# Top-32 attention and a token/channel mixer on one core: the mask of two tiles in three moved to GpSimd as a saturated 0-or-1 word, the dummy values moved to ScalarE

## The chip, the cores and the metric

The kernel runs on 1 core of one Trainium2 chip. The engines of the core are named as the profile names them: PE (TensorE matmul) and PEld (its weight loads), DVE (VectorE), ACT (ScalarE), POOL (GpSimd) and SP (SyncE, which here only issues DMAs). The metric is the device time of one execution in microseconds (us). All inputs and outputs are float32; the kernel itself uses float32 for the scores and bfloat16 behind them.

## The reference

For 8 batches of 8 heads, with 576 positions and a head width of 64:

```python
scores = scale * np.matmul(q, k.transpose(0, 1, 3, 2))        # 576 x 576 per head
kth = np.partition(scores, -32, axis=-1)[..., -32:-31]
mask = scores >= kth
attn = softmax of the masked scores
x = np.matmul(attn, v)                                        # heads side by side: 576 x 512 per batch
h = np.maximum(x.T @ w_tok1, 0.0) @ w_tok2
u = x + h.T
out = u + np.maximum(u @ w_ch1, 0.0) @ w_ch2
```

So each row of scores keeps its 32 largest, takes the exponentials of these, normalises and mixes the values. Two small networks follow, one along the positions and one along the channels.

## The kernel before

**Tiles.** Two heads make a pair; a pair has 9 tiles of 128 score rows by 576 columns (four for each head, and one that holds the last 64 rows of both). 32 pairs make 288 tiles. After the fourth pair of a batch the mixer of that batch (`mlp_ops`) is put beside the attention of the next batch.

**A tile** (`tile_ops`, from line 441) goes round the engines:
- PE makes the scores (L370, L362 for the tile of the last rows) into a two-bank PSUM tile, `big`, of which there are three. ACT copies them to `Ssb` in SBUF (L447), of which there are eight.
- DVE takes the 8 largest of each of seven segments (L452) and reduces these candidates in five steps (L457 to L467) to `thi`, whose last entry is the 24th largest candidate: a first bound for the 32nd score.
- ACT writes `sg`, the sign of (bound - score), and with it the sum of the signs, `cnt` (L469 and its accumulator read). From `cnt` follows how many scores (24 to 31) lie above the bound.
- POOL writes `X` = score times sign (L473), in which the scores above the bound are negative.
- DVE writes the dummy values behind the 576 scores of `X` (L475): nine values, of which as many are +2^100 as the rank needs, the others very negative. The 8 largest of scores and dummies (L479, over 588 columns) then end in the exact 32nd score, `tlo`.
- The mask takes one of three forms, chosen by the tile's number modulo 9:

```python
form = (0, 0, 1, 0, 0, 2, 0, 0, 1)[i % 9]
```

Form 0 (192 tiles): ACT puts the exponential into a PSUM tile `big` (L484), and DVE compares and multiplies in one instruction (L486). Form 1 (64 tiles): ACT puts the exponential into `E` in SBUF (L490), DVE makes the negated bound `nt` (L494), POOL makes the mask in two passes, `Z` (L497: subtract and scale by 2^100) and `M` (L500: cut to 0 and 1), and multiplies (L507). Form 2 (32 tiles): POOL compares in one pass (L504) and multiplies (L507).
- SP issues a DMA transpose of the result `Pm` to `PT` (L509). When a head has its five, PE multiplies by the values (L400) and DVE normalises (L420 to L432).

**Order of the work.** Nothing is ordered while the kernel runs. `Plan` is a list scheduler that is run when the kernel is built: every operation is added with its engine, an assumed duration, a due time in units of `T` (3.1 us a tile), the operations it depends on and the buffers it takes and frees. `Plan.run` simulates the engines and gives one order, in which all instructions are issued; each engine then works through its own queue in that order and waits where data or a buffer isn't there. The loads of a pair are due 16 `T` ahead of it.

**At the end** DVE checks over all tiles that the counts and bounds were as assumed (L618 to L635). If not, an exact version of the whole (`exact_batch`) runs over the output.

Of the kernel before, what the change touches and what calls it, by code (L numbers as in the profile page):

```python
# [7 lines left out]

P = 128
TOPK = 32  # L10
NEG = -1.0e30
BIG = float(2.0**100)

CUT = 8396807.0 / 8388608.0
NSEG = 7
RANK_BASE = 24
NDUM = 9


class Buf:  # L20
# [135 lines left out]
def kernel(  # L156
# [23 lines left out]
    scale = 1.0 / float(D) ** 0.5  # L180
# [3 lines left out]
    ST = S - SM  # L184
    NPAIR = B * H // 2
    NT = NPAIR * 9
    XW = S + 12
    bounds = [round(i * S / NSEG) for i in range(NSEG + 1)]

    main = ExitStack()  # L190
# [3 lines left out]
    def sbt(name, shape, dt):  # L194
        return sb.tile(shape, dt, name=name, tag=name)
# [4 lines left out]
    plan = Plan()  # L200

    def slots(tag, n, shape, dt, psum=False):
        ts = [(pst if psum else sbt)(f"{tag}{i}", shape, dt) for i in range(n)]
        plan.tag(tag, ts)
        return ts

    identF = sbt("identF", [P, P], f32)
    identB = sbt("identB", [P, P], bf16)
    kdum = sbt("kdum", [P, 3, 4], f32)
    w1b = sbt("w1b", [P, 5, DT], bf16)  # L210
    w2b = sbt("w2b", [P, NJ, S], bf16)
    wc1b = sbt("wc1b", [P, NC, DC], bf16)
# [13 lines left out]
    slots("cd", 4, [P, NSEG, 8], f32)  # L226
    slots("m8", 6, [P, 8], f32)
    slots("nt", 4, [P, 1], f32)
    slots("Z", 2, [P, S], f32)
    slots("sg", 3, [P, S], bf16)  # L230
    Xs = slots("X", 4, [P, XW], f32)
    slots("M", 4, [P, S], bf16)
    Ps = slots("Pm", 4, [P, 5 * P], bf16)
    slots("PT", 18, [P, 5, P], bf16)
    slots("rd", 2, [P, 2, 5], f32)
# [11 lines left out]
    make_identity(nc, identF[:, :])  # L247
    nc.vector.tensor_copy(out=identB[:, :], in_=identF[:, :])
    for j in range(NDUM):
        nc.vector.memset(kdum[:, j // 3, j % 3 : j % 3 + 1], float(2 * (j + 1) - 529))  # L250
    for t in Xs:
        nc.vector.memset(t[:, S:XW], -BIG)
    for t in qLs:
        nc.vector.memset(t[:, 4, :, :], 0.0)
    for t in vbs:
# [1 line left out]
    for t in Ps:  # L257
        nc.vector.memset(t[:, S : 5 * P], 0.0)

    T = 3.1  # L260

    def load_w():
        nc.gpsimd.dma_start(
# [20 lines left out]
    def pair_ops(p):  # L284
        b, h0 = divmod(p, 4)
        h0 *= 2
        t0 = 9 * p * T
        qL, kL, vL, vb = Buf("qL"), Buf("kL"), Buf("vL"), Buf("vb")
        qT, kT = Buf("qT"), Buf("kT")
# [31 lines left out]
        pq, pk = Buf("big"), Buf("big")  # L321
# [12 lines left out]

        tt = t0 - 6 * T
        oq = plan.add("PE", 0.6, tt, tr(pq, qL, 5), [lq], acq=[pq, qT], use=[qL])
        ok = plan.add("PE", 0.6, tt + 0.5 * T, tr(pk, kL, 4), [lk], acq=[pk, kT], use=[kL])

        def cp(dst, src, n):
            return lambda: nc.scalar.copy(out=dst.t[:, 0:n], in_=src.t[:, 0:n])  # L340

        eq = plan.add("ACT", 0.65, tt + T, cp(qT, pq, 5 * P), [oq], use=[pq, qT])
        ek = plan.add("ACT", 0.6, tt + 1.5 * T, cp(kT, pk, S), [ok], use=[pk, kT])

        def cv():
            nc.scalar.copy(
# [61 lines left out]
        X = xb[b]  # L408
        tv = t0 + (9 + 5) * T
        for h in range(2):  # L410
# [26 lines left out]
            acq = [rd]  # L437
# [3 lines left out]
    def tile_ops(i, s, S_, om):  # L441

        E, cd, m8 = Buf("E"), Buf("cd"), Buf("m8")
        sg, X, M, Pm, PT = Buf("sg"), Buf("X"), Buf("M"), Buf("Pm"), Buf("PT")
        t = T * i

        ev = plan.add("ACT", 0.6, t + 0.6 * T, lambda: nc.scalar.copy(out=S_.t[:, :], in_=s.t[:, 0:S]),  # L447
                      [om], use=[s, S_])
        last = None
        segs = []  # L450
        for a in range(NSEG):
            segs.append(plan.add("DVE", 0.146, t + T + 0.01 * a, lambda a=a: nc.vector.max(  # L452
                cd.t[:, a, :], S_.t[:, bounds[a] : bounds[a + 1]]), [ev], acq=[cd] if a == 0 else [], use=[S_, cd]))
        d = segs

        def r1():
            nc.vector.max(m8.t[:, :], cd.t[:, :, 0:2])  # L457

        def cut(n):
            return lambda: nc.vector.match_replace(cd.t[:, :, 0:n], m8.t[:, :], cd.t[:, :, 0:n], NEG)  # L460

        tr = t + 1.6 * T
        a1 = plan.add("DVE", 0.085, tr, r1, d, acq=[m8], use=[cd])
        a2 = plan.add("DVE", 0.15, tr + .01, cut(2), [a1], use=[cd, m8])
        a3 = plan.add("DVE", 0.1, tr + .02, lambda: nc.vector.max(m8.t[:, :], cd.t[:, :, 0:5]), [a2], use=[cd, m8])
        a4 = plan.add("DVE", 0.17, tr + .03, cut(5), [a3], use=[cd, m8])
        a5 = plan.add("DVE", 0.125, tr + .04, lambda: nc.vector.max(thi[:, i, :], cd.t[:, :, :]), [a4], use=[cd])  # L467

        ct = plan.add("ACT", 0.77, t + 2.2 * T, lambda: nc.scalar.activation(  # L469
            out=sg.t[:, :], in_=S_.t[:, :], func=AF.Sign, scale=-CUT, bias=thi[:, i, 7:8],  # L470
            accum_out=cnt[:, i : i + 1]), [a5], acq=[sg], use=[S_])

        xm = plan.add("POOL", 1.31, t + 2.7 * T, lambda: nc.gpsimd.tensor_tensor(  # L473
            out=X.t[:, 0:S], in0=S_.t[:, :], in1=sg.t[:, :], op=ALU.mult), [ct], acq=[X], use=[S_, sg])
        dm = plan.add("DVE", 0.09, t + 3.3 * T, lambda: nc.vector.tensor_scalar(  # L475
            out=X.t[:, S:XW].rearrange("p (a b) -> p a b", a=3)[:, :, 0:3], in0=kdum[:, :, 0:3],
            scalar1=cnt[:, i : i + 1], scalar2=-BIG, op0=ALU.add, op1=ALU.mult), [ct, xm], use=[X])

        m = plan.add("DVE", 0.68, t + 3.4 * T, lambda: nc.vector.max(tlo[:, i, :], X.t[:, 0:XW]), [dm, xm], use=[X])  # L479
        thr = tlo[:, i, 7:8]  # L480
        form = (0, 0, 1, 0, 0, 2, 0, 0, 1)[i % 9]
        if form == 0:
            Ep = Buf("big")
            ex = plan.add("ACT", 0.6, t + 3.2 * T, lambda: nc.scalar.activation(  # L484
                out=Ep.t[:, 0:S], in_=S_.t[:, :], func=AF.Exp, scale=scale), [ev, xm], acq=[Ep], use=[S_])
            pm = plan.add("DVE", 0.7, t + 3.6 * T, lambda: nc.vector.scalar_tensor_tensor(  # L486
                out=Pm.t[:, 0:S], in0=S_.t[:, :], scalar=thr, in1=Ep.t[:, 0:S], op0=ALU.is_ge, op1=ALU.mult),
                [m, ex], acq=[Pm], use=[S_, Ep])
        else:
            ex = plan.add("ACT", 0.6, t + 2.4 * T, lambda: nc.scalar.activation(  # L490
                out=E.t[:, :], in_=S_.t[:, :], func=AF.Exp, scale=scale), [ev], acq=[E], use=[S_])
            if form == 1:
                nt, Z = Buf("nt"), Buf("Z")
                tn = plan.add("DVE", 0.07, t + 3.5 * T, lambda: nc.vector.tensor_scalar(  # L494
                    out=nt.t[:, :], in0=thr, scalar1=-(1.0 - 2.0**-24), scalar2=None, op0=ALU.mult),
                    [m], acq=[nt])
                z = plan.add("POOL", 0.8, t + 3.7 * T, lambda: nc.gpsimd.tensor_scalar(  # L497
                    out=Z.t[:, :], in0=S_.t[:, :], scalar1=nt.t[:, :], scalar2=BIG, op0=ALU.add, op1=ALU.mult),
                    [tn], acq=[Z], use=[S_, nt])
                mk = plan.add("POOL", 0.8, t + 3.71 * T, lambda: nc.gpsimd.tensor_scalar(  # L500
                    out=M.t[:, :], in0=Z.t[:, :], scalar1=1.0, scalar2=0.0, op0=ALU.min, op1=ALU.max),
                    [z], acq=[M], use=[Z])
            else:
                mk = plan.add("POOL", 2.0, t + 3.7 * T, lambda: nc.gpsimd.tensor_scalar(  # L504
                    out=M.t[:, :], in0=S_.t[:, :], scalar1=thr, scalar2=None, op0=ALU.is_ge),
                    [m], acq=[M], use=[S_])
            pm = plan.add("POOL", 1.31, t + 3.9 * T, lambda: nc.gpsimd.tensor_tensor(  # L507
                out=Pm.t[:, 0:S], in0=E.t[:, :], in1=M.t[:, :], op=ALU.mult), [mk, ex], acq=[Pm], use=[E, M])
        dt = plan.add("SP", 0.06, t + 4.5 * T, lambda: nc.sync.dma_start_transpose(  # L509
            out=PT.t[:, :, :], in_=Pm.t[:, :]), [pm], acq=[PT], use=[Pm], dma=1.3)  # L510
        return PT, dt
# [96 lines left out]
    for o in order:  # L608
# [4 lines left out]
    tmp = sbt("tmp", [P, NT], f32)  # L613
# [8 lines left out]
                                   op0=ALU.mult, op1=ALU.not_equal)  # L622
# [3 lines left out]
    nc.vector.tensor_reduce(out=bad[:, 1:2], in_=tmp[:, :], op=ALU.max, axis=AX.X)  # L626
    nc.vector.tensor_scalar(out=bad[:, 1:2], in0=bad[:, 1:2], scalar1=56.0, scalar2=None, op0=ALU.is_gt)
    nc.vector.tensor_tensor(out=tmp[:, :], in0=thi[:, :, 7], in1=tlo[:, :, 7], op=ALU.is_gt)
    nc.vector.scalar_tensor_tensor(out=tmp[:, :], in0=tlo[:, :, 7], scalar=0.0, in1=tmp[:, :],
                                   op0=ALU.is_gt, op1=ALU.mult)  # L630
    nc.vector.tensor_reduce(out=bad[:, 2:3], in_=tmp[:, :], op=ALU.min, axis=AX.X)
    nc.vector.tensor_scalar(out=bad[:, 2:3], in0=bad[:, 2:3], scalar1=0.5, scalar2=None, op0=ALU.is_lt)
# [7 lines left out]
    def exact_batch(b, pools):  # L640
        sp, pp = pools
        Xb = sp.tile([P, 5, C], bf16, name="fX", tag="fX")
        for h in range(H):
# [24 lines left out]
            for t in range(5):  # L668
# [92 lines left out]
    with tc.If(wrong > 0):  # L761
        with ExitStack() as fs:
# [10 lines left out]
                out=fw1[:, 0:4, :], in_=moe_w_tok1[0:SM, :].rearrange("(t p) c -> p t c", p=P)  # L773
# [39 lines left out]
```

## Time and profile before

| what | value |
|---|---|
| median of 2 runs | 1094.57 us (1092.71 to 1096.43) |
| the profiled execution's own time | 1090.94 us |
| its span, from the first to the last instruction | 1089.2 us |
| mean granted TensorE clock | 0.761 |
| HBM read, written | 35.78 MB, 9.44 MB |
| longest group of waits, POOL's product L473 for ACT's sign L469 | 333.2 us, 176 times |
| ACT's sign L469 for DVE's bound `thi` L467 | 170.7 us, 163 times |
| PE's score matmuls L370 for ACT's copy L447, for DVE's L486 | 67.2 us, 46.5 us |
| DVE's segment maxima L452 for ACT's copy L447 | 28.5 us, of which 26.8 is the start |

A group's line in the profile gives the line of the kernel, the engine, the operation, what it writes and reads, the shapes and the count; behind the first bar stand the busy time in us and the mean duration of one in ns, behind the second the idle time of the engine just before it and what ended it. Durations of neighbouring instructions on DVE and ACT overlap, so that a group's durations can add up to more than the engine's busy time. In the order of time each line has the start, the duration, and the instruction. The idle time of an engine that doesn't set the end costs nothing.

### The profile page before, as it was taken

The numbers are of one execution on the slowest core, as the hardware profiler recorded it, in microseconds if no ns is written. First come the engines' busy times: TensorE is split into PE (matmuls) and PEld (weight loads), VectorE is DVE, ScalarE is ACT, GpSimd is POOL, SyncE is SP. The second block draws the span as 40 slices with busy tenths as digits, with TensorE's granted clock in tenths as the row PEclk, the third lists the DMA queues.
The fourth block names the chain that finished last, engine by engine and source line by source line (L and its number), as shares of the span: only waits on it lengthen the run. The fifth ranks groups of instructions, "written<-read, shape, count | busy, mean of one in ns | idle before, by whom it ended". The sixth has DMA issues, their size and how long they took to land. (4 is left out here: it accounts for less than half of the span.)

```text
span 1089.2 us, 19075 instructions
## 1 busy us (share of the span) xinstructions
PE 834.2 (77%) x4804; PEld 480.0 (44%) x4850; DVE 988.6 (91%) x5094; ACT 735.6 (68%) x1465; POOL 636.0 (58%) x555
## 2 busy tenths in 40 slices
PE   2776678888789588897689876887787975798377
PEld 1443444555444354544455443444444543454233
DVE  0889999999999989999999999999999999999920
ACT  0766666876687766876678766787668866787422
POOL 1366666666765655566666665566556665665600
PEclk9756557995599755996589965898569966798578
DMA  9644334454435534454443543345434433234201
GB/s 178 134 67 88 82 76 82 71 118 87 74 63 103 106 74 73 61 119 83 80 82 66 130 83 65 71 92 109 88 62 79 100 86 77 44 48 97 51 13 48
DMA packets 317192, 90.04 MB, mean 83 GB/s; under 512 B 309968, under 2 KB 311824, under 8 KB 317072
## 3 DMA queue, kind: packets, MB, share of 16 engines
q1 hardware_dynamic: 314496, 84.99, 39.9%
q0 software_dynamic: 2576, 3.74, 1.9%
q8 instruction: 40, 0.66, 0.2%
q14 instruction: 80, 0.66, 0.2%
HBM read 35.78 MB, written 9.44 MB: 42 GB/s over the span
## 5 line engine op out<-in xcount | busy, mean ns | idle before, releaser
L473 POOL TENSOR_TENSOR X<-Ssb,sg 128x576 f32<-128x576 f32 x288 | 367.7, 1279 | 333.9 <-ACT sg L469 333.2
L452 DVE MAX8 cd<-Ssb 128x8 f32<-128x82 f32 (+1 forms) x2016 | 382.0, 230 | 28.6 <-ACT Ssb L447 28.5
L370 PE MATMUL big<-kT,qT 64*128 64x512 f32 (+1 forms) x1024 | 301.5, 588 | 116.6 <-ACT Ssb L447 67.2
L469 ACT ACTIVATE sg<-Ssb,thi 128x576 bf16<-128x576 f32 x288 | 223.0, 774 | 209.9 <-DVE thi L467 170.7
L370 PEld LDWEIGHTS big<-kT,qT 64*128 64x128 f32 x1024 | 160.4, 250 | 252.3 <-ACT Ssb L447 85.1
L479 DVE MAX8 tlo<-X 128x8 f32<-128x588 f32 x288 | 222.1, 771 | 5.3 <-DVE m L457 0.4
L400 PE MATMUL one<-vb,PT 128*128 128x65 bf16 (+2 forms) x1600 | 146.6, 223 | 58.9 <-DMA PT<-Pm 56.4
L447 ACT COPY Ssb<-big 128x576 f32<-128x576 f32 x288 | 172.4, 634 | 24.9 <-PE big L370 15.1
L486 DVE SCALAR_TENSOR_TENSOR Pm<-Ssb,tlo,big 128x576 bf16<-128x576 f32 x192 | 155.7, 812 | 8.2 <-ACT big L484 0.8
L400 PEld LDWEIGHTS <-PT 128*128 128x128 bf16 (+2 forms) x1600 | 102.0, 111 | 102.8 <-DMA PT<-Pm 58.5
L475 DVE TENSOR_SCALAR X<-kdum,cnt 128x9 f32<-128x9 f32 x288 | 125.6, 436 | 2.7 <-ACT sg L469 2.6
L507 POOL TENSOR_TENSOR Pm<-E,M 128x576 bf16<-128x576 bf16 x96 | 122.5, 1276 | 7.8
L570 PE MATMUL big<-UT,wc1b 128*128 128x64 bf16 (+1 forms) x744 | 104.2, 287 | 27.5 <-ACT H L576 11.2
L484 ACT ACTIVATE big<-Ssb 128x576 f32<-128x576 f32 x192 | 124.2, 649 | 1.3 <-DVE Pm L486 1.0
L585 PE MATMUL one<-wc2b,H 128*128 128x512 bf16 (+1 forms) x466 | 111.5, 382 | 3.5 <-ACT ob L598 1.8
L460 DVE MATCH_REPLACE8 cd<-m,cd 128x14 f32<-128x14 f32 (+1 forms) x576 | 97.1, 169 | 0.0
L570 PEld LDWEIGHTS <-wc1b 128*128 128x128 bf16 x768 | 53.2, 99 | 77.6 <-issue 32.0
L497 POOL TENSOR_SCALAR Z<-Ssb,nt 128x576 f32<-128x576 f32 x64 | 47.8, 748 | 45.9 <-DVE nt L494 44.2
L585 PEld LDWEIGHTS <-H 128*128 128x128 bf16 (+1 forms) x480 | 45.2, 101 | 48.5 <-issue 3.5
L576 ACT ACTIVATE H<-big 128x576 bf16<-128x576 f32 x96 | 59.3, 643 | 9.4 <-PE big L570 9.3
L490 ACT ACTIVATE E<-Ssb 128x576 bf16<-128x576 f32 x96 | 64.6, 677 | 0.9
L362 PE MATMUL big<-kT,qT 128*128 128x64 f32 (+1 forms) x128 | 52.8, 545 | 11.2 <-ACT Ssb L447 6.6
(72 smaller groups left out, 849.8 us busy)
## 6 DMA issues: line engine op xcount, KB each, us to landing
qL<-in_q_dram SPq DMA_DIRECT2D x64, 128.0 KB, 2.7
kL<-in_k_dram SPq DMA_DIRECT2D x64, 128.0 KB, 2.7
vL<-in_v_dram SPq DMA_DIRECT2D x64, 128.0 KB, 2.7
out_dram<-ob SPq DMA_DIRECT2D x32, 256.0 KB, 2.3
PT<-Pm SPq DMA_TRANSPOSE x288, 2.6
wc1b<-in_moe_w_ch_dram POOLq DMA_DIRECT2D x1, 1536.0 KB, 14.0
wc2b<-in_moe_w_ch_dram POOLq DMA_DIRECT2D x1, 1536.0 KB, 23.3
qL<-in_q_dram SPq DMA_DIRECT2D x64, 16.0 KB, 2.3
```

The lines of the kernel that those rows point to most:

```text
L370: nc.tensor.matmul(out=bs[h].t[:, lo:hi], lhsT=qT.t[r, g * P : (g + 1) * P], rhs=kT.t[r, lo:hi], start=True, stop=True,)
L400: nc.tensor.matmul(out=o[0:m, g, :], lhsT=src[0:kr, j, cs], rhs=vb.t[0:kr, j, h, :], start=(j == 0), stop=(j == 4),)
L447: ev = plan.add("ACT", 0.6, t + 0.6 * T, lambda: nc.scalar.copy(out=S_.t[:, :], in_=s.t[:, 0:S]), [om], use=[s, S_])
L452: segs.append(plan.add("DVE", 0.146, t + T + 0.01 * a, lambda a=a: nc.vector.max(cd.t[:, a, :], S_.t[:, bounds[a] : bounds[a + 1]]), [ev], ...
L469: ct = plan.add("ACT", 0.77, t + 2.2 * T, lambda: nc.scalar.activation(out=sg.t[:, :], in_=S_.t[:, :], func=AF.Sign, scale=-CUT, bias=thi[ ...
L473: xm = plan.add("POOL", 1.31, t + 2.7 * T, lambda: nc.gpsimd.tensor_tensor(out=X.t[:, 0:S], in0=S_.t[:, :], in1=sg.t[:, :], op=ALU.mult), ...
L475: dm = plan.add("DVE", 0.09, t + 3.3 * T, lambda: nc.vector.tensor_scalar(out=X.t[:, S:XW].rearrange("p (a b) -> p a b", a=3)[:, :, 0:3], ...
L479: m = plan.add("DVE", 0.68, t + 3.4 * T, lambda: nc.vector.max(tlo[:, i, :], X.t[:, 0:XW]), [dm, xm], use=[X])
L484: ex = plan.add("ACT", 0.6, t + 3.2 * T, lambda: nc.scalar.activation(out=Ep.t[:, 0:S], in_=S_.t[:, :], func=AF.Exp, scale=scale), [ev, xm ...
L486: pm = plan.add("DVE", 0.7, t + 3.6 * T, lambda: nc.vector.scalar_tensor_tensor(out=Pm.t[:, 0:S], in0=S_.t[:, :], scalar=thr, in1=Ep.t[:, ...
L570: nc.tensor.matmul(out=pb.t[:, lo:hi], lhsT=wc1b[:, cc, fc * P : (fc + 1) * P], rhs=UT.t[:, cc, lo:hi], start=(cc == 0), stop=(cc == NC - 1))
L585: nc.tensor.matmul(out=pb.t[0:r, 0:C], lhsT=H2.t[:, fc, cs], rhs=wc2b[:, fc, :], start=(fc == 0), stop=False)
```

## The change

- The scores are kept times 2^80: ACT multiplies the transposed q by it when it copies it from PSUM, and the exponentials divide by it again through their scale. The constants for "very large" and "very small" and the check's lower limit follow.
- The dummy values are written by ACT instead of DVE: one `activation` with function Copy, scale `cnt` and a constant bias, over seven prepared constants instead of nine, behind the accumulator read in ACT's queue. `X` is 583 columns wide instead of 588, and its padding isn't filled at the start any more.
- The forms are two now: two tiles in three (192) go through POOL, one in three (96) through DVE's L486. On POOL the mask is one pass: score plus negated bound, cut above at 16256, written as uint16. A negative value becomes 0; 16256 is the bit pattern of 1.0 in bfloat16, and the multiplication reads the word as bfloat16. `Z` is gone, `M` has three slots instead of four. L504's form is gone.
- `T` is 2.85 instead of 3.1, and some assumed durations differ, so all queues are ordered anew.

```diff
-NEG = -1.0e30
-BIG = float(2.0**100)
+UP = float(2.0**80)
+LOW = float(2.0**40)
+ONE = 16256.0
+NEG = -float(2.0**120)
+BIG = float(2.0**120)
...
-NDUM = 9
+NDUM = 7
...
-    XW = S + 12
+    XW = S + NDUM
...
-    slots("Z", 2, [P, S], f32)
...
-    slots("M", 4, [P, S], bf16)
+    slots("M", 3, [P, S], u16)
...
-        nc.vector.memset(kdum[:, j // 3, j % 3 : j % 3 + 1], float(2 * (j + 1) - 529))
-    for t in Xs:
-        nc.vector.memset(t[:, S:XW], -BIG)
+        nc.vector.memset(kdum[:, j : j + 1], BIG / float(2 * (j + 1) - 529))
...
-    T = 3.1
+    T = 2.85
...
-        def cp(dst, src, n):
-            return lambda: nc.scalar.copy(out=dst.t[:, 0:n], in_=src.t[:, 0:n])
+        def cp(dst, src, n, by):
+            return lambda: nc.scalar.activation(
+                out=dst.t[:, 0:n], in_=src.t[:, 0:n], func=AF.Copy, scale=by)
...
-        eq = plan.add("ACT", 0.65, tt + T, cp(qT, pq, 5 * P), [oq], use=[pq, qT])
+        eq = plan.add("ACT", 0.65, tt + T, cp(qT, pq, 5 * P, UP), [oq], use=[pq, qT])
...
-        ev = plan.add("ACT", 0.6, t + 0.6 * T, lambda: nc.scalar.copy(out=S_.t[:, :], in_=s.t[:, 0:S]),
+        ev = plan.add("ACT", 0.54, t + 0.6 * T, lambda: nc.scalar.copy(out=S_.t[:, :], in_=s.t[:, 0:S]),
...
-        dm = plan.add("DVE", 0.09, t + 3.3 * T, lambda: nc.vector.tensor_scalar(
-            out=X.t[:, S:XW].rearrange("p (a b) -> p a b", a=3)[:, :, 0:3], in0=kdum[:, :, 0:3],
-            scalar1=cnt[:, i : i + 1], scalar2=-BIG, op0=ALU.add, op1=ALU.mult), [ct, xm], use=[X])
+        dm = plan.add("ACT", 0.2, t + 2.9 * T, lambda: nc.scalar.activation(
+            out=X.t[:, S:XW], in_=kdum[:, :], func=AF.Copy, scale=cnt[:, i : i + 1], bias=BIG), [ct], use=[X])
...
-        form = (0, 0, 1, 0, 0, 2, 0, 0, 1)[i % 9]
+        form = (1, 1, 0, 1, 1, 0, 1, 1, 0)[i % 9]
...
-                z = plan.add("POOL", 0.8, t + 3.7 * T, lambda: nc.gpsimd.tensor_scalar(
-                    out=Z.t[:, :], in0=S_.t[:, :], scalar1=nt.t[:, :], scalar2=BIG, op0=ALU.add, op1=ALU.mult),
-                    [tn], acq=[Z], use=[S_, nt])
-                mk = plan.add("POOL", 0.8, t + 3.71 * T, lambda: nc.gpsimd.tensor_scalar(
-                    out=M.t[:, :], in0=Z.t[:, :], scalar1=1.0, scalar2=0.0, op0=ALU.min, op1=ALU.max),
-                    [z], acq=[M], use=[Z])
-            else:
-                mk = plan.add("POOL", 2.0, t + 3.7 * T, lambda: nc.gpsimd.tensor_scalar(
-                    out=M.t[:, :], in0=S_.t[:, :], scalar1=thr, scalar2=None, op0=ALU.is_ge),
-                    [m], acq=[M], use=[S_])
+                mk = plan.add("POOL", 0.76, t + 3.7 * T, lambda: nc.gpsimd.tensor_scalar(
+                    out=M.t[:, :], in0=S_.t[:, :], scalar1=nt.t[:, :], scalar2=ONE, op0=ALU.add, op1=ALU.min),
+                    [tn], acq=[M], use=[S_, nt])
             pm = plan.add("POOL", 1.31, t + 3.9 * T, lambda: nc.gpsimd.tensor_tensor(
-                out=Pm.t[:, 0:S], in0=E.t[:, :], in1=M.t[:, :], op=ALU.mult), [mk, ex], acq=[Pm], use=[E, M])
+                out=Pm.t[:, 0:S], in0=E.t[:, :], in1=M.t[:, :].bitcast(bf16), op=ALU.mult), [mk, ex], acq=[Pm], use=[E, M])
```

More of the change, by code (lines that the diff above doesn't have):

```diff
@@ L171 @@
     i32 = mybir.dt.int32
+    u16 = mybir.dt.uint16
     AF = mybir.ActivationFunctionType
@@ L208 @@
     identB = sbt("identB", [P, P], bf16)
-    kdum = sbt("kdum", [P, 3, 4], f32)
+    kdum = sbt("kdum", [P, NDUM], f32)
     w1b = sbt("w1b", [P, 5, DT], bf16)
@@ L337, in pair_ops @@
         ok = plan.add("PE", 0.6, tt + 0.5 * T, tr(pk, kL, 4), [lk], acq=[pk, kT], use=[kL])
-        def cp(dst, src, n):
-            return lambda: nc.scalar.copy(out=dst.t[:, 0:n], in_=src.t[:, 0:n])
-        eq = plan.add("ACT", 0.65, tt + T, cp(qT, pq, 5 * P), [oq], use=[pq, qT])
-        ek = plan.add("ACT", 0.6, tt + 1.5 * T, cp(kT, pk, S), [ok], use=[pk, kT])
+        def cp(dst, src, n, by):
+            return lambda: nc.scalar.activation(
+                out=dst.t[:, 0:n], in_=src.t[:, 0:n], func=AF.Copy, scale=by)
+        eq = plan.add("ACT", 0.65, tt + T, cp(qT, pq, 5 * P, UP), [oq], use=[pq, qT])
+        ek = plan.add("ACT", 0.6, tt + 1.5 * T, cp(kT, pk, S, 1.0), [ok], use=[pk, kT])
         def cv():
@@ L484, in tile_ops @@
             ex = plan.add("ACT", 0.6, t + 3.2 * T, lambda: nc.scalar.activation(
-                out=Ep.t[:, 0:S], in_=S_.t[:, :], func=AF.Exp, scale=scale), [ev, xm], acq=[Ep], use=[S_])
+                out=Ep.t[:, 0:S], in_=S_.t[:, :], func=AF.Exp, scale=scale / UP), [ev, xm], acq=[Ep], use=[S_])
             pm = plan.add("DVE", 0.7, t + 3.6 * T, lambda: nc.vector.scalar_tensor_tensor(
@@ L490, in tile_ops @@
             ex = plan.add("ACT", 0.6, t + 2.4 * T, lambda: nc.scalar.activation(
-                out=E.t[:, :], in_=S_.t[:, :], func=AF.Exp, scale=scale), [ev], acq=[E], use=[S_])
+                out=E.t[:, :], in_=S_.t[:, :], func=AF.Exp, scale=scale / UP), [ev], acq=[E], use=[S_])
             if form == 1:
-                nt, Z = Buf("nt"), Buf("Z")
-                tn = plan.add("DVE", 0.07, t + 3.5 * T, lambda: nc.vector.tensor_scalar(
+                nt = Buf("nt")
+                tn = plan.add("DVE", 0.08, t + 3.5 * T, lambda: nc.vector.tensor_scalar(
                     out=nt.t[:, :], in0=thr, scalar1=-(1.0 - 2.0**-24), scalar2=None, op0=ALU.mult),
                     [m], acq=[nt])
-                z = plan.add("POOL", 0.8, t + 3.7 * T, lambda: nc.gpsimd.tensor_scalar(
-                    out=Z.t[:, :], in0=S_.t[:, :], scalar1=nt.t[:, :], scalar2=BIG, op0=ALU.add, op1=ALU.mult),
-                    [tn], acq=[Z], use=[S_, nt])
-                mk = plan.add("POOL", 0.8, t + 3.71 * T, lambda: nc.gpsimd.tensor_scalar(
-                    out=M.t[:, :], in0=Z.t[:, :], scalar1=1.0, scalar2=0.0, op0=ALU.min, op1=ALU.max),
-                    [z], acq=[M], use=[Z])
-            else:
-                mk = plan.add("POOL", 2.0, t + 3.7 * T, lambda: nc.gpsimd.tensor_scalar(
-                    out=M.t[:, :], in0=S_.t[:, :], scalar1=thr, scalar2=None, op0=ALU.is_ge),
-                    [m], acq=[M], use=[S_])
+                mk = plan.add("POOL", 0.76, t + 3.7 * T, lambda: nc.gpsimd.tensor_scalar(
+                    out=M.t[:, :], in0=S_.t[:, :], scalar1=nt.t[:, :], scalar2=ONE, op0=ALU.add, op1=ALU.min),
+                    [tn], acq=[M], use=[S_, nt])
             pm = plan.add("POOL", 1.31, t + 3.9 * T, lambda: nc.gpsimd.tensor_tensor(
-                out=Pm.t[:, 0:S], in0=E.t[:, :], in1=M.t[:, :], op=ALU.mult), [mk, ex], acq=[Pm], use=[E, M])
+                out=Pm.t[:, 0:S], in0=E.t[:, :], in1=M.t[:, :].bitcast(bf16), op=ALU.mult), [mk, ex], acq=[Pm], use=[E, M])
         dt = plan.add("SP", 0.06, t + 4.5 * T, lambda: nc.sync.dma_start_transpose(
@@ L628 @@
     nc.vector.tensor_tensor(out=tmp[:, :], in0=thi[:, :, 7], in1=tlo[:, :, 7], op=ALU.is_gt)
-    nc.vector.scalar_tensor_tensor(out=tmp[:, :], in0=tlo[:, :, 7], scalar=0.0, in1=tmp[:, :],
+    nc.vector.scalar_tensor_tensor(out=tmp[:, :], in0=tlo[:, :, 7], scalar=LOW, in1=tmp[:, :],
                                    op0=ALU.is_gt, op1=ALU.mult)
```

## The prediction

> **What bounds the kernel now.** I read the page's busy shares first, then three stretches of the span, then the groups with shapes kept apart, then the order of time on DVE and POOL, then short stretches of high and of low TensorE clock.
>
> ```profile
> span 1089.2 us, 19075 instructions
> PE 834.2 (77%) x4804; PEld 480.0 (44%) x4850; DVE 988.6 (91%) x5094; ACT 735.6 (68%) x1465; POOL 636.0 (58%) x555
> ```
>
> The same by stretch (columns: the stretch, its length, then PE, PEld, DVE, ACT, POOL busy, granted clock, DMA share, GB/s):
>
> ```profile
> 0.00:28.90 28.90, 7.64 (x22) 4.15 (x22) 1.11 (x24) 3.68 (x6) 4.54 (x11) 1.00 1.02 179
> 28.90:1035.80 1006.90, 788.28 (x4532) 455.89 (x4574) 981.27 (x5050) 717.47 (x1437) 628.82 (x541) 0.75 0.42 83
> 1035.80:1089.20 53.40, 38.23 (x250) 19.96 (x254) 6.24 (x21) 14.49 (x23) 2.69 (x3) 0.82 0.10 31
> ```
>
> The reader is to see a head of 28.9 us (loads), a middle of 1006.9 us in which DVE is idle for only 25.6, and a tail of 53.4 us (the last batch's mixer). So DVE's work sets the middle. The next engines there are PE at 78%, ACT at 71%, POOL at 62%.
>
> The groups that the change touches (columns: busy us, mean ns of one; idle before):
>
> ```profile
> L473 POOL TENSOR_TENSOR X<-Ssb,sg 128x576 f32<-128x576 f32 x288 | 367.7, 1279 | 333.9 <-ACT sg L469 333.2
> L475 DVE TENSOR_SCALAR X<-kdum,cnt 128x9 f32<-128x9 f32 x288 | 125.6, 436 | 2.7 <-ACT sg L469 2.6
> L486 DVE SCALAR_TENSOR_TENSOR Pm<-Ssb,tlo,big 128x576 bf16<-128x576 f32 x192 | 155.7, 812 | 8.2 <-ACT big L484 0.8 <-DVE cd L460 0.4
> L494 DVE TENSOR_SCALAR nt<-tlo 128x1 f32<-128x1 f32 x64 | 9.3, 146 | 0.0
> L504 POOL TENSOR_SCALAR M<-Ssb,tlo 128x576 bf16<-128x576 f32 x32 | 55.3, 1727 | 8.9 <-DVE tlo L479 8.9
> L507 POOL TENSOR_TENSOR Pm<-E,M 128x576 bf16<-128x576 bf16 x96 | 122.5, 1276 | 7.8
> ```
>
> L475 writes nine elements and yet takes 436 ns on the mean. Its tile view gives 201/215/1346 (min/median/max), so a stall sits inside some. The order of time shows it:
>
> ```profile
> 512.82 1.28 POOL L473 TENSOR_TENSOR X<-Ssb,sg 128x576 f32<-128x576 f32 x1 [0.23 <-ACT sg L469]
> 513.13 0.99 DVE L475 TENSOR_SCALAR X<-kdum,cnt 128x9 f32<-128x9 f32 x1
> 514.04 0.18 DVE L465 MAX8 m<-cd 128x8 f32<-128x35 f32 x1
> ```
>
> L475 starts inside a POOL instruction and ends just after it. Of the 108 that took over 260 ns, 101 ended 20 to 30 ns after the end of a POOL instruction; their excess over 215 ns is 64 us. In 98 of the 108 the tile's own product (L473) was already done, so this isn't a wait for data. L494, also a TENSOR_SCALAR, is never held: 28 of its 64 began during an L473, 14 with over 0.3 us of it left, and none of the 64 took over 155 ns.
>
> **The change, part by part** (middle only, unless said). DVE's instructions overlap, so I cost each by the time from its start to the next DVE start, from the trace's order.
>
> *L475 leaves DVE.* Start to next start: median 125 ns, mean 349, so 288 x 0.349 = 100.6 us, of which 288 x 0.224 = 64.5 is the stall. Less could go: in the 10 long cases whose product was not done, and in others as narrow, L479 would wait for L473 itself; summed over all tiles, L475 starts 7.3 us too early. So 93 to 100.6; I take 100.6.
>
> *96 of 192 L486 leave DVE.* 729 ns start to start: 96 x 0.729 = 70.0 us.
>
> *L494 goes from 64 to 192.* Median 61 ns: 128 x 0.061 = 7.8 us. From above, were it held as L475 is: 192 x 0.224 = 43 more; the unheld rows speak against that.
>
> *L479 reads 583 elements for 588:* 5 x 1.07 ns (from 771 at 588 against 229 at 82) x 288 = 1.5 us.
>
> DVE after: 981.3 - 100.6 - 70.0 + 7.8 - 1.5 = 817 us, that is 0.570 us less per tile.
>
> *The dummy write comes to ACT,* 288 times, and no row shows it. Below: an accumulator read's start-to-start, 93 ns (27 us in all). Above: L349's whole duration, 299 ns (86 us). I build it: L349 (128 elements) goes start to start in 0.199, L346 (512) in 0.507, so 0.80 ns an element and 0.102 at seven; a pointer operand adds 0.093 (L469 with one against L490 without, 665 and 572 at least). 0.195 x 288 = 56 us. ACT after: 717.5 + 56 = 773. The 96 exps that change from PSUM to SBUF have the same spacing of 572, and the 64 copies that gain a scale 5 ns each (643 against 638): 0.3 us in all, taken as nothing.
>
> *A new wait:* L479 on DVE now needs ACT's dummy write as well as POOL's product. ACT does it in its own order, behind copies and exps of other tiles; behind L479 on DVE stand the seven maxima of the next tiles, then thi, then ACT's sign. In the plan it is due 0.5 T before L479, and POOL's product takes 1.28 us meanwhile: I take nothing, and give the loss to a rival.
>
> *POOL.* The mask is now one pass with pointer and immediate, 192 times. L497 (pointer and immediate) takes 748, L500 (two immediates) 667, L504's compare 1727. It is nearest L497 in form; the uint16 output is unseen. I take 748 and keep 667 and 1727. The three passes of a masked tile follow each other with gaps:
>
> ```profile
> 508.50 0.75 POOL L497 TENSOR_SCALAR Z<-Ssb,nt 128x576 f32<-128x576 f32 x1 [1.85 <-DVE nt L494]
> 509.33 0.67 POOL L500 TENSOR_SCALAR M<-Z 128x576 bf16<-128x576 f32 x1
> 510.08 1.27 POOL L507 TENSOR_TENSOR Pm<-E,M 128x576 bf16<-128x576 bf16 x1
> ```
>
> 0.085 us from one to the next. POOL after: 367.7 + 192 x (0.748 + 0.085 + 1.276) = 773 us, 0.47 more per tile than 636.
>
> [...]
>
> *SP* issues the same 288 transposes and loads in one queue; two in three now wait for POOL's L507 instead of DVE's L486, with loads queued behind. Loads run 16 T ahead: nothing. *Slots:* Z goes; M has three instead of four, written and read by POOL in order: nothing. Fewer exps hold a big buffer (96 for 192), which loosens PE's wait on L486 (46.5 us): below nothing, but PE isn't the bound, so I take zero. *Head:* two constant writes and four fills fewer (0.25 us), under the loads. *Tail:* the last tile is masked on DVE instead of POOL's chain, 2 us sooner at most; zero taken. *T* from 3.1 to 2.85 and the new durations reorder every queue; the trace can't price that. It gains 25.6 at most, and its loss is in the idle below.
>
> **Which engine is next.** With 0.570 off DVE per tile, 0.195 on ACT and 0.47 on POOL, stretches differ (two with the clock high, two low; tiles by L475's count are 21, 22, 15 and 15):
>
> ```profile
> 309.00:380.00 71.00, 55.87 (x365) 30.16 (x369) 70.22 (x348) 54.05 (x108) 43.19 (x37) 0.93 0.48 89
> 565.00:636.00 71.00, 57.68 (x381) 31.28 (x386) 69.91 (x367) 56.12 (x113) 45.84 (x41) 0.93 0.45 95
> 254.00:309.00 55.00, 44.98 (x230) 28.72 (x231) 54.16 (x286) 37.84 (x77) 36.17 (x32) 0.60 0.43 81
> 510.00:565.00 55.00, 44.62 (x225) 28.39 (x227) 54.15 (x287) 37.55 (x77) 35.77 (x31) 0.60 0.41 76
> ```
>
> High clock, 142 us, 43 tiles, mixer work on: DVE 140.1 - 24.5 = 115.6; ACT 110.2 + 8.4 = 118.6; PE 113.6; POOL 89.0 + 20.2 = 109.2. Low clock, 110 us, 30 tiles: DVE 108.3 - 17.1 = 91.2; PE 89.6; POOL 86.0; ACT 81.2. The largest of each: 209.8 of 252, so the middle's floor is 0.8325 x 1006.9 = 838 us. All four engines stand close to it.
>
> [...]
>
> **The sum.** DVE's idle was 25.6 with the next engine at 78%; with four together it must grow. I estimate one and a half times, 38. Middle 838 + 38 = 876; head 28.9; tail 53.4: span 958.3. Around the span the profiled execution had 1.7 us (1090.94 against 1089.2), so 960. That execution lies 3.6 below the median 1094.57, less than the terms are known by.
>
> **Rivals.**
> - *DVE remains alone the bound,* ACT and PE work shifting between stretches: 817 + 25.6 + 82.3 + 1.7 = 927. For it: 817 is above 773 and 773. Against it: the stretch sums. 0.20.
> - *The new wait bites:* the dummy write stands behind one ACT copy (0.64, L447) when DVE is ready. At one tile in three, 96 x 0.64 = 61 more: 1021. For it: L469 already waited 170.7 us for DVE, so the two go back and forth. 0.15.
> - *POOL becomes the bound:* the uint16 pass costs as the compare does, 1727: 367.7 + 192 x 3.088 = 961; with 25.6 + 84.0, 1070. 0.10.
> - *Slower by over 2%,* by POOL's mask pass alone: 1.02 x 1090.9 = 1113 needs 367.7 + 192 x (m + 1.361) = 1003, m = 1.95 us; level with before at 1.83. The dearest one-input pass here is 1.73. 0.04.
> - *The forecast,* 940 to 985: 0.51.
>
> **How the numbers follow.** A measurement tells some 2% (22 us) from no change. The forecast and the first two rivals (0.86) are faster by more. The POOL bound lies at that line (1073) and is split in halves: faster 0.91, same 0.05, slower 0.04. The range leaves out the POOL rivals (0.14) and some edges: 920 to 1030.
>
> **What would show it.** Right: DVE near 825 us over the span, L475 gone from DVE, 96 L486; POOL near 780; a new ACT row of 288, 128x7 and under 0.3 us; L479 without idle before it; no L494 over 0.16. Wrong: mask rows well above 0.75 with DVE waiting for transposed results or slots; idle before L479 put down to ACT (the second rival); L494 held to the ends of POOL instructions; idle on PE in low-clock stretches gone while DVE's rises (PE is the bound). If ACT's dummy row counts 288 but costs over 0.4, ACT is the bound in the mixer's stretches and the time nears 1000.

## The result and the profile after

The changed kernel takes 1158.8 us (median of two runs, 1158.32 to 1159.28): 1.0587 times the time before, with a 95% interval of 1.0507 to 1.0666. The forecast was 960, faster. The time is that of the rival to which the prediction gave 0.04: the mask pass on POOL is dearer than 1.95 us.

The page of the changed kernel, first its busy shares, then the chain that ended last, by engine:

```profile
span 1156.5 us, 19232 instructions
PE 868.3 (75%) x4799; PEld 474.4 (41%) x4850; DVE 819.8 (71%) x4832; ACT 783.2 (68%) x1753; POOL 1023.8 (89%) x683
...
POOL 68%; PE 10%; DVE 7%; DMA 5%; issue 4%; SPq 2%; ACT 2%; POOLq 0%; DVEq 0%; ACTq 0%
```

The same three stretches as before the change (head, middle, tail; columns as there):

```profile
0.00:28.40 28.40, 7.64 (x22) 4.15 (x22) 1.00 (x18) 3.96 (x7) 4.53 (x11) 1.00 1.04 181
28.40:1103.80 1075.40, 820.15 (x4527) 449.27 (x4574) 812.67 (x4794) 764.74 (x1725) 1019.23 (x672) 0.74 0.38 77
1103.80:1156.50 52.70, 40.56 (x250) 21.00 (x254) 6.14 (x21) 14.47 (x23) 0.00 (x0) 0.79 0.10 31
```

The middle is 1075.4 us long, and now it is POOL that is idle for little of it (56 us). DVE did fall as worked out, to 812.7 (817 was forecast), and is idle for 263 us. Head and tail are as they were. The groups, with shapes kept apart, say where POOL's time went and what DVE waits for:

```profile
L500 POOL TENSOR_SCALAR M<-Ssb,nt 128x576 uint16<-128x576 f32 x192 | 423.5, 2206 | 9.0 <-DVE nt L497 7.0 <-DMA kL<-in_k_dram 1.1 <-DMA qL<-in_q_dram 0.2
L477 POOL TENSOR_TENSOR X<-Ssb,sg 128x576 f32<-128x576 f32 x288 | 363.8, 1276 | 58.3 <-ACT sg L473 56.5 <-DMA qL<-in_q_dram 1.7
L503 POOL TENSOR_TENSOR Pm<-E,M 128x576 bf16<-128x576 bf16 x192 | 244.5, 1274 | 11.5
L482 DVE MAX8 tlo<-X 128x8 f32<-128x583 f32 x288 | 219.0, 760 | 228.9 <-POOL X L477 228.8
L479 ACT ACTIVATE X<-kdum,cnt 128x7 f32<-128x7 f32 x288 | 83.5, 295 | 0.1
```

The mask pass L500 takes 2206 ns; the forecast took 748, and kept 1727 as the upper end. L503 and L477 have their old prices. DVE's idle time stands before L482, and POOL's product is what ends it: POOL's queue is late, and DVE stands behind it. With m = 2.206 the prediction's own formula for a POOL bound gives 367.7 + 192 x (2.206 + 1.361) + 25.6 + 84 = 1162, against 1158.8 measured. That the two lie 3 us apart is luck in part: the formula's middle has 1053 us of work and 26 of idle on POOL, the trace 1019 and 56, for neighbouring passes mostly overlap by 20 to 50 ns, and POOL waits longer. But the term that made the forecast miss is the one price. The experiments ask why that pass is dear, whether the other steps hold, and what each part of the change is worth alone.

### The profile page after: what moved, and what is told of

It is laid out like the page before. It is cut to its first block, busy times and chain, and to the rows that moved or that the text cites. A ratio compares the mean times of both kernels' runs of the same rounds, so it can differ in the third digit from the quotient of the medians.

```text
span 1156.5 us, 19232 instructions
## 1 busy us (share of the span) xinstructions
PE 868.3 (75%) x4799; PEld 474.4 (41%) x4850; DVE 819.8 (71%) x4832; ACT 783.2 (68%) x1753; POOL 1023.8 (89%) x683
## 4 chain that ended last, share of the span: by engine, by line
POOL 68%; PE 10%; DVE 7%; DMA 5%; issue 4%; SPq 2%; ACT 2%; POOLq 0%; DVEq 0%; ACTq 0%
POOL M L500 32%; POOL X L477 20%; POOL Pm L503 16%; DVE tlo L482 3%; PE big L374 3%; DMA PT<-Pm 2%; PE one L581 2%; DMA qL<-in_q_dram 2%; PE one L404 2%; PE big L566 1%; DVE cd L456 1%; PE one L527 1%; SPq L313 1%; SPq L297 1%; ACT sg L473 1%
## 5 line engine op out<-in xcount | busy, mean ns | idle before, releaser
L500 POOL TENSOR_SCALAR M<-Ssb,nt 128x576 uint16<-128x576 f32 x192 | 423.5, 2206 | 9.0 <-DVE nt L497 7.0
L456 DVE MAX8 cd<-Ssb 128x8 f32<-128x82 f32 (+1 forms) x2016 | 392.4, 230 | 41.2 <-ACT Ssb L451 40.8
L477 POOL TENSOR_TENSOR X<-Ssb,sg 128x576 f32<-128x576 f32 x288 | 363.8, 1276 | 58.3 <-ACT sg L473 56.5
L482 DVE MAX8 tlo<-X 128x8 f32<-128x583 f32 x288 | 219.0, 760 | 228.9 <-POOL X L477 228.8
L503 POOL TENSOR_TENSOR Pm<-E,M 128x576 bf16<-128x576 bf16 x192 | 244.5, 1274 | 11.5
L374 PEld LDWEIGHTS big<-kT,qT 64*128 64x128 f32 x1024 | 149.2, 252 | 239.1 <-issue 90.7
L581 PE MATMUL one<-wc2b,H 128*128 128x512 bf16 (+1 forms) x460 | 123.2, 409 | 20.0 <-ACT ob L594 11.7
L493 ACT ACTIVATE E<-Ssb 128x576 bf16<-128x576 f32 x192 | 127.0, 678 | 0.4
L479 ACT ACTIVATE X<-kdum,cnt 128x7 f32<-128x7 f32 x288 | 83.5, 295 | 0.1
L489 DVE SCALAR_TENSOR_TENSOR Pm<-Ssb,tlo,big 128x576 bf16<-128x576 f32 x96 | 77.5, 807 | 4.3 <-ACT big L487 2.2
L487 ACT ACTIVATE big<-Ssb 128x576 f32<-128x576 f32 x96 | 62.1, 647 | 2.0 <-DVE Pm L489 1.9
```

Of the source, the lines that this page charges most:

```text
L374: nc.tensor.matmul(out=bs[h].t[:, lo:hi], lhsT=qT.t[r, g * P : (g + 1) * P], rhs=kT.t[r, lo:hi], start=True, stop=True,)
L500: mk = plan.add("POOL", 0.76, t + 3.7 * T, lambda: nc.gpsimd.tensor_scalar(out=M.t[:, :], in0=S_.t[:, :], scalar1=nt.t[:, :], scalar2=ONE, ...
L581: nc.tensor.matmul(out=pb.t[0:r, 0:C], lhsT=H2.t[:, fc, cs], rhs=wc2b[:, fc, :], start=(fc == 0), stop=False)
```

## The experiments

All ratios are to the kernel before on the same chip, which took 1091 to 1093 us there. The fences of edits give the heart of each, most of them in short, and "..." stands for what is left out. A pointer is a scalar that is read from a tile, one value for each partition (such as `nt`); an immediate is a constant.

**The price of the pass, eight forms in one kernel.** The mask pass of the changed kernel was given eight forms in turn:

```diff
-   kind 0 everywhere: (score + nt) min 16256 -> uint16
+   kind 0 as it was; 1 into bf16; 2 into f32; 3 two immediates; 4 min alone;
+   kind 5 into int32; 6 (score * 2**-70) max 0.0 -> uint16; 7 score + nt -> bf16
```

> The 192 mask passes are given eight forms in turn (24 each), so the result is not the mask: (0) uint16 written, pointer add, min, as in the changed kernel; (1) the same, bf16 written; (2) the same, f32 written; (3) uint16, both scalars immediates; (4) uint16, min alone; (5) the same as 0, int32 written; (6) uint16, score times 2^-70, cut below at 0, so that no value is out of range; (7) bf16, pointer add alone. Theory A, writing the integer word makes the pass dear: forms 0, 3, 4, 6 take about 2.2 us, forms 1, 2, 7 0.67 to 0.75 us, form 5 also over 1.5. Rival B, the operations (an add with a pointer, then min) or the large numbers make it dear: forms 1 and 2 take about 2.2 us as well, 4 or 6 less. Rival C, values outside the range make it dear: form 6 takes about 0.75, forms 0, 3, 4 2.2.

Its POOL groups (kinds 5, 0, 2, 1, 6, 3, 7, 4 from the top):

```profile
L517 POOL TENSOR_SCALAR M<-Ssb,nt 128x576 int32<-128x576 f32 x24 | 53.2, 2216 | 0.2 <-DVE nt L497 0.2
L507 POOL TENSOR_SCALAR M<-Ssb,nt 128x576 uint16<-128x576 f32 x24 | 53.1, 2211 | 7.1 <-DVE nt L497 6.9
L511 POOL TENSOR_SCALAR M<-Ssb,nt 128x576 f32<-128x576 f32 x24 | 53.0, 2207 | 1.8 <-DVE nt L497 1.6
L509 POOL TENSOR_SCALAR M<-Ssb,nt 128x576 bf16<-128x576 f32 x24 | 53.0, 2206 | 0.0
L519 POOL TENSOR_SCALAR M<-Ssb 128x576 uint16<-128x576 f32 x24 | 51.4, 2144 | 2.0
L513 POOL TENSOR_SCALAR M<-Ssb 128x576 uint16<-128x576 f32 x24 | 51.2, 2132 | 2.1
L521 POOL TENSOR_SCALAR M<-Ssb,nt 128x576 bf16<-128x576 f32 x24 | 41.6, 1732 | 0.0
L515 POOL TENSOR_SCALAR M<-Ssb 128x576 uint16<-128x576 f32 x24 | 39.7, 1653 | 0.0
```

What is written (int32, uint16, f32, bf16) makes no difference. Values outside the range of the output aren't it either (rival C): bf16 and f32 hold the values that lie outside uint16's range, at the same price (2206 and 2207 for 2211), and kind 6, with no value out of range, takes 2144. My first theory, that the integer output is dear, falls; rival B remains: the operations, or the large numbers. A single operation takes 1653 with an immediate and 1732 with a pointer, a second one adds 0.48 us. The kernel takes 1130 us in one run, with passes that are on the mean cheaper.

**The same from the other side: bfloat16 out.**

```diff
-    slots("M", 3, [P, S], u16)
+    slots("M", 3, [P, S], bf16)
...
```

> The changed kernel, but the mask pass writes bf16 instead of uint16, so that what is written is no longer a 0 or 1 mask. Theory A: the price of this one pass is all that the prediction's sum had wrong: pass 0.75 us, POOL 773 us busy, time 960 (940 to 985). Rival B, the pass is dear whatever it writes: 1150 to 1165. Rival D, other new waits (L482 on DVE for POOL's product, ACT's dummy write) cost as well: pass 0.75 and time over 1000.

1156.6 us, ratio 1.0596 (1.0550 to 1.0641), POOL 1023.7 us busy: nothing changes. That is rival B, by its pass (2206 ns) and by its time.

**The old two passes on two tiles in three.** Add and multiply by 1.0 into f32, then min and max into bf16, as the kernel before did it in form 1:

```diff
+   z:  Z = (score + nt) * 1.0
+   mk: M = max(min(Z, 1.0), 0.0)
```

> The changed kernel with the mask made in two passes by the way of before (f32 in between, then bf16), still on two tiles in three. Theory A: the two passes take 0.75 and 0.67 us and with their gaps POOL has 367.7 + 192 x 2.86 = 917 us of work, which bounds: 917 + 25.6 + 84 = 1027 us (1010 to 1045). Rival B, large numbers make POOL's pass dear: first pass over 1.5 us and 1120 or more. Rival D: over 1060.

```profile
L501 POOL TENSOR_SCALAR Z<-Ssb,nt 128x576 f32<-128x576 f32 x192 | 143.1, 745 | 64.5 <-DVE nt L498 64.1
L504 POOL TENSOR_SCALAR M<-Z 128x576 bf16<-128x576 f32 x192 | 128.0, 667 | 11.3
```

1053.5 us, ratio 0.9641 (0.9600 to 0.9681). Two passes on the same large scores take 1.41 us together, one pass took 2.21: large numbers alone are not the cause, and the pair of operations remains. The time is 26 above the expected, over theory A's range and under rival D's: POOL waits 64 us for `nt`, so POOL alone doesn't bound any more.

**The dummy values on ACT alone.** The kernel before, with its T, forms and mask:

```diff
-   dm on DVE: tensor_scalar(kdum + cnt, * -BIG)
+   dm on ACT: activation(Copy, kdum, scale=cnt, bias=BIG)
```

> The kernel before, with one part of the change alone: the dummy values written by ACT. Theory A (the prediction's step for DVE): 100 us leave DVE, DVE's middle is 880 us and still the largest: 880 + 25.6 + 84 = 990 us (975 to 1010). Rival E, the stall goes to the wait for POOL's product instead: L479 then has some 64 us of idle time before it, 1040 to 1055. Rival F, the dummy write behind ACT's queue makes DVE wait: idle before L479 put down to ACT, over 1020.

1017.6 us, ratio 0.9309 (0.9265 to 0.9352): this part of the change is a gain by itself. DVE's middle falls to 864 us (880 expected), but its idle time there rises from 25 to 67 us, so the time is 28 above the expected 990 and outside its range. Before L476, the maximum that needs the dummies, the idle is 18.7 us, of which ACT's dummy write ended 7.0: neither rival E nor F explains much of it; the idle is spread over the copies, exponentials and products that DVE waits for.

**Twelve pairs of operations.**

```diff
+   pairs by kind: (add n, mult) (min, max) (max, min) (add, add) (mult, add) (mult, mult)
+   (add n, max) (is_ge n, mult) (subtract n, mult) (min, mult) (mult) ; (add, min) on small bf16
```

> The changed kernel with twelve pairs of operations in turn in the mask pass (16 each), all into uint16; the mask is left out of the product, which multiplies E by itself. (0) add pointer, multiply; (1) min, max; (2) max, min; (3) add, add; (4) multiply, add; (5) multiply, multiply; (6) add pointer, max; (7) compare with pointer, multiply; (8) subtract pointer, multiply; (9) min, multiply; (10) multiply alone; (11) add, min on small bfloat16 numbers. Theory G, a few pairs have a fast form and all the rest a slow one: 0 and 1 take 0.67 to 0.75 us, most others 1.65 to 2.2. Rival H, add and multiply are fast in any pair and min, max and compares slow outside (1): 3, 4, 5, 8, 10 at 0.75, 2, 6, 7, 9, 11 at 2.2. Rival I, large numbers make it slow: 11 takes 0.75 or less.

```profile
L521 POOL TENSOR_SCALAR M<-Ssb,nt 128x576 uint16<-128x576 f32 x16 | 35.5, 2221 | 0.1
L523 POOL TENSOR_SCALAR M<-Ssb,nt 128x576 uint16<-128x576 f32 x16 | 35.5, 2217 | 3.3 <-DVE nt L497 2.9 <-DVE cd L456 0.3
L519 POOL TENSOR_SCALAR M<-Ssb,nt 128x576 uint16<-128x576 f32 x16 | 35.4, 2213 | 6.4 <-DVE nt L497 4.9 <-DVE cd L456 1.3
L513 POOL TENSOR_SCALAR M<-Ssb 128x576 uint16<-128x576 f32 x16 | 34.5, 2156 | 0.0
L529 POOL TENSOR_SCALAR M<-E 128x576 uint16<-128x576 bf16 x16 | 34.3, 2144 | 0.0
L525 POOL TENSOR_SCALAR M<-Ssb 128x576 uint16<-128x576 f32 x16 | 34.2, 2137 | 0.0
L511 POOL TENSOR_SCALAR M<-Ssb 128x576 uint16<-128x576 f32 x16 | 34.1, 2134 | 0.0
L527 POOL TENSOR_SCALAR M<-Ssb 128x576 uint16<-128x576 f32 x16 | 26.6, 1662 | 0.0
L507 POOL TENSOR_SCALAR M<-Ssb,nt 128x576 uint16<-128x576 f32 x16 | 12.0, 748 | 1.8 <-DVE nt L497 1.3
L515 POOL TENSOR_SCALAR M<-Ssb 128x576 uint16<-128x576 f32 x16 | 10.8, 675 | 0.0
L517 POOL TENSOR_SCALAR M<-Ssb 128x576 uint16<-128x576 f32 x16 | 10.8, 675 | 0.0
L509 POOL TENSOR_SCALAR M<-Ssb 128x576 uint16<-128x576 f32 x16 | 10.7, 667 | 0.0
```

There are two classes, up to 748 ns and from 1662, with nothing in between. Cheap: add and multiply (L507), multiply and add (L515), multiply and multiply (L517), min and max (L509). Dear: all others, the single multiplication too (L527), among them max and min (L511), which differs from L509 only in the order, add and add (L513), subtract and multiply (L523), compare and multiply (L521), and add and min on small bfloat16 numbers (L529). Theory G holds, and H and I fall. The kernel takes 1045.9 us in one run.

**Types, pointers and more pairs.**

```diff
+   (min, max) into bf16, f32; (max, min), (add, add), (min, min), (mult, subtract) into bf16; (mult) into f32
+   (min n, max), (min n, max n), (add n, mult) into bf16; (min, max) on bf16 into uint16 and bf16
```

> A second list of twelve forms of the mask pass (16 each; the mask is left out of the product, which multiplies E by itself). On the f32 scores: (0) min, max into bfloat16; (1) min, max into f32; (2) max, min into bfloat16; (3) add, add into bfloat16; (6) add pointer, multiply into bfloat16; (7) min, min into bfloat16; (8) min pointer, max into bfloat16; (9) min pointer, max pointer into bfloat16; (10) multiply, subtract into bfloat16; (11) multiply alone into f32. On the bfloat16 exponentials: (4) min, max into uint16; (5) min, max into bfloat16. Theory G2, min with max has a fast form for float outputs only: 0, 1, 5 at 0.67, 4 at 2.1, and 2 and 8 tell whether the order and a pointer matter; 3, 7, 10, 11 at 1.65 to 2.2, 6 at 0.75. Rival M, the input decides (the fast one before read small cut numbers): 0 and 1 at 2.1, 5 at 0.67.

Min with max takes 664 to 667 ns from f32 or bfloat16 into bfloat16, f32 or uint16, 740 with one pointer and 811 with two; add with multiply 745 into bfloat16. Max with min takes 2138, add with add 2149, min with min 2143, multiply with subtract 2153, multiply alone 1652. So neither type decides: rival M falls, and so does G2's condition on the output, while the rest of G2 stands, and a pointer costs 0.07 to 0.08 us in both classes. The kernel takes 1005.8 us in one run, with five of twelve passes dear.

**A one-pass mask from a cheap pair.** Add and multiply can't cut at the top, so the cut is left to the int8 word that is written, the upper byte of a bfloat16:

```diff
-   out=M, (score + nt) min 16256
+   out=M as int8, every second byte, (score + nt) * 1.0
...
+   v and its column of ones times 2**-100
```

> The changed kernel with another one-pass mask: score plus negated bound, times 1.0 (add, then multiply, the operations of the pass that took 0.748 us before), written as int8 into the upper byte of a bfloat16 word whose lower byte is zero: 127 there is a large finite number, -128 is -0, 0 is 0; the values and the column of ones are scaled by 2^-100, and the normalisation takes the factor out. Theory G, the pair (add, min) alone was dear: pass 0.75 us, POOL 773 us busy, DVE 820; with DVE's idle as in the last two runs (some 60 us) 817 + 60 + 84 = 961 us (940 to 985), where the prediction had put the change. Rival K, the strided bytes are dear: pass over 1.2 us, time over 1000. Rival D, waits between the engines cost more once POOL is free: pass 0.75 and over 1000.

970.1 us, ratio 0.8897 (0.8865 to 0.8928), against both kernels a gain. The pass takes 747 ns, and the middle follows it:

```profile
L503 POOL TENSOR_SCALAR M<-Ssb,nt 128x576 int8<-128x576 f32 x192 | 143.5, 747 | 24.9 <-DVE nt L500 23.9
28.60:916.60 888.00, 754.21 (x4574) 429.88 (x4574) 807.52 (x4794) 757.77 (x1725) 742.55 (x672) 0.81 0.48 94
```

With the pass at its assumed price, the prediction's sum is nearly met: middle 888 against 876, time 970 against 960. So the price of the pass is what made the changed kernel slow. The small miss hides two larger ones: 817 us of work on DVE in a middle of 876 left it 59 us of idle (21 up to the floor of 838, and the 38), and the trace has 80 of idle and 807.5 of work.

**Two passes, fewer tiles.**

```diff
-    T = 2.85
+    T = 2.95
...
-        form = (1, 1, 0, 1, 1, 0, 1, 1, 0)[i % 9]
+        form = (1, 0, 1, 0, 1, 0, 1, 0, 0)[i % 9]
...
```

> As the run with two passes on POOL, but four tiles in nine (128) masked there instead of six, and T 2.95. POOL's work 367.7 + 128 x 2.86 = 734 us; DVE 817 + 64 x (0.729 - 0.061) = 860. Theory A (the sums, with some 60 us of idle on DVE): 860 + 60 + 84 = 1004 us (985 to 1020), faster than both runs with two passes or with the old shares. Rival D, the idle grows with every engine that comes near DVE: 1020 to 1050.

1022.6 us, ratio 0.9351 (0.9302 to 0.9400), at the lower edge of rival D. DVE has 850 us in the middle and 93 idle, POOL 704. With two passes, then, four tiles in nine on POOL give no gain over the dummies on ACT with the old shares and forms (1017.6).

**The mask part alone.** The changed kernel, with the dummies on DVE:

> The changed kernel with the dummy values put back on DVE, so that the mask, the shares and T are the part of the change that is left. Theory A: POOL bounds with 1052 us of work, DVE has slack: 1155 to 1175 if L475 stays at 436 ns. Theory L, L475 is held until the running POOL instruction ends: with POOL busy for most of the middle L475's mean rises to 700 to 1000 ns, DVE's busy time to over 950, and the time to 1165 to 1230. Rival E, L475's stall was a wait for the tile's own product: the mean stays at or under 436 and the time at 1160.

```profile
L485 DVE MAX8 tlo<-X 128x8 f32<-128x588 f32 x288 | 222.1, 771 | 103.8 <-POOL X L479 100.1
L481 DVE TENSOR_SCALAR X<-kdum,cnt 128x9 f32<-128x9 f32 x288 | 160.6, 558 | 0.1
```

1150.7 us, ratio 1.0529 (1.0474 to 1.0584). DVE's write is held longer, 558 ns for 436, DVE is busy for 962 us, and none of it counts, since POOL bounds. Theory L named the direction, but 558 is under its 700, and the time lies under the range of every theory (1155 and more): of the 164 writes over 260 ns only 10 began in the 2.2 us pass. Of these, 8 were let go 0.76 us after the pass began, not at its end; the other two began late in it and were held to its end. 103 more began in that pass and were not held. In the changed kernel, then, the dummies on ACT are worth nothing, though alone they gain 73 us.

**The stall, by one address pattern.** The kernel before, with nine constants side by side:

```diff
-    kdum = sbt("kdum", [P, 3, 4], f32)
+    kdum = sbt("kdum", [P, 9], f32)
...
-            out=X.t[:, S:XW].rearrange("p (a b) -> p a b", a=3)[:, :, 0:3], in0=kdum[:, :, 0:3],
+            out=X.t[:, S:XW].rearrange("p (a b) -> p a b", a=3)[:, :, 0:3], in0=kdum[:, :].rearrange("p (a b) -> p a b", a=3),
```

> The kernel before, with the nine constants lying side by side instead of three and three with a gap, so that L475 reads one run of nine and writes three runs of three; nothing else differs. [...] Rival N, any such write by DVE is held: L475's mean stays near 436 and the time at 1090.

```profile
L475 DVE TENSOR_SCALAR X<-kdum,cnt x288: 191/204/223, 35.1 to 985.4; 128x9 f32<-128x9 f32 x144
```

1040.6 us, ratio 0.9517 (0.9467 to 0.9566). The same nine values are written by the same instruction, and only the way the constants are read differs. The mean falls from 436 to 205 ns and no case is over 223 (1346 before), though 94 of the writes began with over 0.3 us of a POOL instruction left, and DVE is busy for 926 us instead of 989. Rival N falls: how the constants are read decides. Three by three on both sides was held, nine against three by three was not. The two runs don't tell the shape of the read from the gap between its rows of three, which went with it, and they don't show by what POOL holds the write.

**The best mask with the dummies back on DVE, in that form.** The one-pass mask was run again beside it:

> The one-pass mask by add and multiply once more, beside the next kernel on the same chip: 970 us (965 to 975).

> The same, but the dummy values written by DVE in the form that POOL does not hold (nine constants side by side), so that ACT's 288 writes are gone. DVE has 817 + 288 x 0.125 = 853 us, ACT 718. Theory A (DVE's work sets the middle, with its idle): with the 80 us of idle seen, 853 + 80 + 82 = 1015 us. Rival P, several engines share the bound and ACT's work counts as well: DVE's idle falls by what ACT is given, and the time stays within 965 to 985.

969.3 us, ratio 0.8871 (0.8843 to 0.8898), and 987.3 us, 0.9037 (0.9008 to 0.9066). With the dummies on DVE its middle has 859 us of work and 43 idle; on ACT 807 and 85 (81 in the run before). Rival P is nearer: most of DVE's 52 us more went into waits that were there anyway. 18 us of the time remain by the medians, 2 us past P's edge, and 10 between these two middles, of which the one on ACT is from an execution 7 us above its median.

## Why the prediction was wrong

**The step that failed** is the price of the mask pass: "It is nearest L497 in form; the uint16 output is unseen. I take 748 and keep 667 and 1727." Form was judged by operands (a pointer and an immediate), and doubt was put on the output type. Neither decides. L497 adds and multiplies, the new pass adds and takes a minimum, and that pair belongs to the dear class: 2206 ns. The upper end was no bound either: 1727 was a pass with one operation, and a second costs 0.48 more. The page before held the hint, a compare with less to do (L504) that took 2.3 times as long as L497; I read it as a property of the compare. The 192 passes cost 192 x 1.458 = 280 us more on POOL than taken.

**The rival's chance.** Break-even stood at 1.83 us and slower by 2% at 1.95, with the dearest row at 1.73: margins of 0.1 and 0.2 us on a price that no row showed. 0.04 was too little.

**L475 leaves DVE, and its stall is POOL's hold:** right. DVE's middle is 812.7 for 817 forecast; alone, the hold is worth 51 us of time (1091.9 to 1040.6) and the whole step 73 (1090.9 to 1017.6). **L486 halved, L494 tripled:** right; L494 was never held (147 ns on the mean, 156 at most in the changed kernel).

**The dummy write on ACT:** right, 191 to 202 ns from start to start on the median in these runs, for 195. **The new wait** on it costs nothing in the changed kernel: of 228.9 us of idle before L482, POOL's product ended 228.8. With POOL not in the way it shows, but far under the rival's 61 us: ACT's write ended 2.5 us of the idle in the kernel of 970 us, 7.0 with the dummies alone, and 16.0 with four tiles in nine. **Gaps between POOL's passes, head, tail:** right within 5 us each.

**Which engine is next, and the idle:** right in kind, too small in size. With the pass at its assumed price the time was 970 for 960, but DVE had 80 us of idle for the 59 left to it, and 10 us less work made up for half of that. In other shares DVE's idle rose to 67 (dummies on ACT) and to 93 (four tiles in nine), where the expectations had 25.6 and 60.

**POOL's price for a masked tile** is above DVE's even with the cheap pair, 0.747 + 1.274 us on POOL for 0.81 on DVE. But there POOL doesn't set the end (742.6 us busy in a middle of 888), and the one-pass mask, the shares and `T` together take the time from 1017.6 (dummies on ACT) to 970.1, 5% less. With the dear pair POOL sets the end (1019.2 us busy in a middle of 1075.4).

**Still open:** why just these four pairs are cheap. The runs show the classes, not what POOL executes. And DVE's 80 us of idle in the fastest kernel were not tested: its trace puts 28 before L485 (most of them ended by POOL's product), 21 before L492 (ACT's exponential), some 17 before the segment maxima (ACT's copy) and 11 before the normalisation (PE). All four engines are busy for 77 to 84% of its span.

## What to carry to other kernels

The price of a TENSOR_SCALAR on GpSimd went here, at one size, by the exact pair of operations in their order, not by the types or by how many operations there are: take it from a row with the same pair, or measure it in a list of forms inside one kernel before moving work there. When work moves to an engine, work out the price at which that engine sets the end, and if an unseen price lies within some tenths of a microsecond of it, give that case a real chance. A short instruction with a long mean is worth a look at its minimum and at what ended when it ended: here one address pattern was worth 5% of the time.

## What the runs showed of the hardware

- On GpSimd, 128x576, add with multiply, multiply with add, multiply with multiply and min with max took 664 to 748 ns (811 with two pointers); all other pairs tried took 2132 to 2221, single operations 1652 to 1732. A single multiplication takes 2.5 times as long as two (1662 against 675, both into uint16).
- A strided int8 output cost GpSimd nothing: 747 ns into every second byte, 745 to 748 for the same pair of operations into bf16, f32 or uint16 side by side.
- A DVE write of nine elements, three by three on both sides, waited for running GpSimd instructions (101 of 108 long cases ended 20 to 30 ns after one); with its source read as one run of nine, it didn't (205 ns on the mean and 223 at most in the kernel of 1040.6 us, 204 on the mean in that of 987.3).
- A dear GpSimd pass held such a write for a part of its time: 8 of 10 were let go 0.76 us after the 2.2 us pass began, and in the kernel before 7 of 9 as long after the 1.7 us compare began. The other four were let go 20 to 30 ns after its end.
